# Linear attention and two MLPs on one core: a reciprocal-root activation in place of Ln and Exp, a shorter norm step, and four of the second batch's products in plain float32

## The chip, the cores and the metric

The kernel runs on one core of a Trainium2 chip. The metric is the device time of one execution in microseconds (us), the median of the runs shown. Matmuls run on TensorE (PE), whose weight loads are listed apart (PEld). VectorE (DVE) and ScalarE (ACT) do the elementwise work and read the matmul results out of PSUM, GpSimd (POOL) does very little here, and SyncE (SP) issues most of the DMAs.

## The reference

```python
def _attn_ref(q, k, v, g_norm):                 # 8 batches, 8 heads, 576 tokens, head_dim 64
    kv = np.einsum('bhsd,bhse->bhde', k, v)
    out = np.einsum('bhsd,bhde->bhse', q, kv)
    rms = np.sqrt(np.mean(out * out, axis=-1, keepdims=True) + 1e-06)
    return (out / rms * g_norm).astype(np.float32)

def _moe_ref(x, w_in, w_out):                   # 4608 tokens, 512 -> 2048 -> 512
    h = x @ w_in
    beta = 1.0
    ...
    g = np.where(pos, h, np.where(neg, 0.0, (h + beta) ** 2 / (4.0 * beta)))
    return (g @ w_out).astype(np.float32)

def _moe2_ref(x, w_in, w_out):                  # the same sizes
    h = x @ w_in
    r = np.maximum(h, 0.0)
    g = r * r
    return (g @ w_out).astype(np.float32)
...
    x = np.ascontiguousarray(attn_out.transpose(0, 2, 1, 3)).reshape(B * S, H * D)
    x = _moe_ref(x=x, **moe_kwargs)
    return _moe2_ref(x=x, **moe2_kwargs)
```

The weights arrive as float64 words and are narrowed to float32 inside the kernel.

## The kernel before

A float32 product is made of three matmuls of a rounded type (float32r): each operand is split into a rounded part (hi) and the rest (lo), and `mm3` (L235 to L238) multiplies hi by hi, hi by lo and lo by hi into one PSUM bank. ACT casts the hi part, DVE subtracts it to get the lo part (`split`, L228 to L230; for weights L185).

The tokens are taken in blocks of 512 and, for layer 1, block b holds the tokens of batch b. A block has 16 steps f of 128 hidden units. `h_stage` multiplies x by `w_0_f` into `ph_b_f` (12 matmuls of 128x512), ACT and DVE make u from it (L705, L224, L707), `gs_b_f` is its split, and `out_stage` multiplies gs by `w_1_f` into four accumulators (`acc_b_0` to `acc_b_3`, 12 matmuls). Two PSUM banks named "h" take turns for ph. In block 0 each weight piece is narrowed just before it is used: ACT scales `raw` (L268), DVE builds the bits `d` (L270, L271), ACT casts `w` (L217) and DVE subtracts (L185).

Attention works on pairs of heads, four to a batch: k and v to `pkv` (L479), a transposed q times the kept kv matrix to `po` (two halves of 288 columns), squares of po, their sums over a head by a matmul with `ones` into `pr`, and the norm in `r_first` (batch 0) or `r_stage` (the others). There, ACT takes Ln of each half of pr from PSUM (L535, L602) and one Exp over 576 columns with scale -0.5 (L537, L604), so that y is a reciprocal root. ACT squares it into t (L224). DVE multiplies t by pr + 1e-6 (`newton`, L519, a half at a time); `norm` then forms (t - 3)*y (L522) and multiplies by o, the product scaled by g (L523). The result is split into the block's x.

Batch 0's attention runs ahead of everything; dummy matmuls (`pwarm`, L1157) stand between its steps on PE. The attention of batch b is hooked into block b-1, a pair about every seven steps, so batch 1's pairs 0 to 3 stand in block 0. For pairs 0 and 1 of batch 1 (`WHOLE`, L109) q and kv stay in plain float32 (L569, tile `kvw`) and so does the sum of squares; pairs 2 and 3 use the three-product form with `kvbd`. After the blocks of layer 1 come the passes of the rest, from about 714 us on.

The order of the instructions on each engine is set by a scheduler when the program is built; each engine takes its own in order. So an instruction that is added, taken out or released at another time in the schedule can change what stands beside it.

Of the kernel before, what the change touches and what calls it, by code (L numbers as in the profile page):

```python
# [15 lines left out]
BF16 = mybir.dt.bfloat16  # L16

LN_SCALE = 2.0**-44  # L20
LN2 = 0.6931471805599453

# [53 lines left out]
def linear_attention_rms_two_mlps(  # L78
# [16 lines left out]
    P = 128  # L95
# [12 lines left out]
    WAVE = 6  # L108
    WHOLE = ((1, 0), (1, 1))  # L109
    WARMS = ((0, 5), (6, 5), (8, 3), (12, 4), (14, 3), (20, 3), (26, 3))  # L110
    SPLITS = (10, 15, 24, 29, 32, 33)
# [77 lines left out]
    gvec = const.tile([P, 1], F32, name="gvec")  # L189
    lnb = const.tile([P, 1], F32, name="lnb")  # L190
    expb = const.tile([P, 1], F32, name="expb")
    halfb = const.tile([P, 1], F32, name="halfb")
# [274 lines left out]
    def kv_stage(b, *hps):  # L467
# [12 lines left out]
        for n, hp in enumerate(hps):  # L480
            for j in range(2):
                s = slice(j * D, (j + 1) * D)
                d = slice(n * P + j * D, n * P + (j + 1) * D)
                if b == 0:
                    copy(engine("kv_hi", b), kv0[s, hp, s], ps[s, d])
                    continue
                if (b, hp) in WHOLE:
                    copy(engine("kv_hi", b), kvw[s, hp % 2, s], ps[s, d])
                    continue
                t = kvbd[turn[b, hp] % len(kvbd)]  # L490
                copy(engine("kv_hi", b), t[s, 0, s], ps[s, d])
                nc.vector.tensor_tensor(t[s, 1, s], ps[s, d], t[s, 0, s].bitcast(F32), ALU.subtract)
# [27 lines left out]

    def norm(t, y, o):
        nc.vector.scalar_tensor_tensor(t, t, -3.0, y, op0=ALU.add, op1=ALU.mult)  # L522
        nc.vector.tensor_tensor(t, o, t, ALU.mult)  # L523

    marks = []

    def r_first(hp):
# [3 lines left out]
        for half in range(2):  # L531
            ps = bank(0, f"pr_0_{hp}_{half}")
            m = ps[:, :U]
            nc.tensor.matmul(m, ones.bitcast(F32), y[:, half], start=True, stop=True)  # L534
            nc.scalar.activation(y[:, half], m, AF.Ln, bias=lnb, scale=LN_SCALE)  # L535
            ms.append(m)
        nc.scalar.activation(y, y, AF.Exp, bias=expb, scale=-0.5)  # L537
        square(engine("y", 0), t, y)
        for half in range(2):
            newton(t[:, half], ms[half])  # L540
        norm(t, y, o)
        n = TB // 2
# [6 lines left out]
    def t_stage(b, hp):  # L549
        work = [ap1.tile([P, S], F32, tag=f"wk{n}", name=f"wk{n}_{b}_{hp}") for n in range(2)]  # L550
        if (b, hp) in WHOLE:
            qT = ap1.tile([P, S], F32, tag="hl0", name=f"qT_{b}_{hp}")
            nc.vector.transpose(qT, qs.pop((b, hp)))
            hl[b, hp] = (work, qT)
            return
# [7 lines left out]
    def o_stage(b, hp, half):  # L563
        work, parts = hl[b, hp]
        kv = kvbd[turn[b, hp] % len(kvbd)]
        c = slice(half * U, (half + 1) * U)
        if (b, hp) in WHOLE:
            ps = bank(b, f"po_{b}_{hp}_{half}")
            nc.tensor.matmul(  # L569
                ps[:, :U], kvw[:, hp % 2, :], parts[:, c], start=True, stop=True  # L570
            )
            nc.scalar.activation(work[0][:, c], ps[:, :U], AF.Square)
            scaled(engine("o", b), work[1][:, c], ps[:, :U], gvec)
            return
# [3 lines left out]
        s2 = og[b, hp]  # L578
        ps = bank(b, f"po_{b}_{hp}_{half}")
        mm3(ps[:, :U], lambda a: kv[:, a, :], lambda a: parts[a][:, c], True, True)  # L580
        nc.scalar.activation(s2[0][:, c], ps[:, :U], AF.Square)
        nc.scalar.activation(work[0][:, c], ps[:, :U], AF.Square)
        scaled(engine("o", b), work[1][:, c], ps[:, :U], gvec)
        if half == 1:
            s2.append(ap1.tile([P, S], F32R, tag="hl1", name=f"s2lo_{b}_{hp}"))
            lo = engine("sq_lo", b)
            lo.tensor_tensor(s2[1], work[0], s2[0].bitcast(F32), ALU.subtract)

    def r_stage(b, hp):
# [6 lines left out]
        for half in range(2):  # L596
# [3 lines left out]
            for n, (one, s2) in enumerate(products):  # L600
                nc.tensor.matmul(m, one, s2[:, c], start=n == 0, stop=n == len(products) - 1)  # L601
            nc.scalar.activation(y[:, c], m, AF.Ln, bias=lnb, scale=LN_SCALE)  # L602
            ms.append((c, m))
        nc.scalar.activation(y, y, AF.Exp, bias=expb, scale=-0.5)  # L604
        t = ap1.tile([P, S], F32, tag="wk2", name=f"t_{b}_{hp}")
        square(engine("y", b), t, y)
        for c, m in ms:
            newton(t[:, c], m)
        if b < LAST_B:
            norm(t, y, o)  # L610
            nc.gpsimd.tensor_copy(xrem[b][:, hp, :], t[:, TB:])
            split(xs[1, b][hp], t[:, :TB], "x", b)
            return
        xt = st.tile([P, TB], F32, tag="st", name=f"xt_{hp}")
        nc.vector.scalar_tensor_tensor(t, t, -3.0, y, op0=ALU.add, op1=ALU.mult)
        nc.vector.tensor_tensor(xt, o[:, :TB], t[:, :TB], ALU.mult)
        nc.vector.tensor_tensor(xrem[b][:, hp, :], o[:, TB:], t[:, TB:], ALU.mult)
        x_kept[hp] = xt
# [526 lines left out]

    nc.scalar.preload_act_table_set("natural_log_exp_and_others")
    load_first()
# [22 lines left out]
    nc.vector.tensor_scalar_mul(gvec, gvec, -0.5)  # L1170
    nc.vector.memset(lnb, LN_SCALE * 1e-6)
    nc.vector.memset(expb, -22.0 * LN2)
    nc.vector.memset(halfb, 0.5)
# [121 lines left out]
```

## Time and profile before

| | before |
|---|---|
| runs | 1556.57, 1558.22, 1556.27 us; median 1556.57 |
| profiled execution, its own time | 1556.74 us |
| its span | 1554.7 us |
| PE busy | 1545.8 us, 99% |
| DVE busy | 1131.3 us, 73% |
| ACT busy | 909.6 us, 59% |

The span is from the first to the last recorded work; some 2 us of the execution's time lie outside it. An engine that is busy for 99% of the span can get shorter only where it waits or by doing less. Where a wait is listed, the bracket behind a row gives the idle time before it and the engine and line that ended it. Consecutive instructions of an engine overlap, so the pitch (start to start) is less than the duration of one.

### The profile page before, as it was taken

Reading aid. Unit: us, or ns where it says so; the run is one execution under the profiler, and the core shown is the slowest. Engines: PE = TensorE matmul, PEld = TensorE weight load, DVE = VectorE, ACT = ScalarE, POOL = GpSimd, SP = SyncE. Lnnn points to the kernel's source line nnn. Section 1 sums busy time; section 2 is a strip of 40 time slices with the busy share of each in tenths; the row PEclk is TensorE's granted clock in tenths of the full one; section 3 lists DMA queues with packets and bytes.
Section 4 is the critical chain, followed back from the end, with each engine's and each line's share of the span. In section 5 each row is a group of like instructions: output and inputs, shape, how many; then the busy total and the mean of one; then the engine's idle time right before and its main releaser. Section 6 shows DMA issues by size and latency. Waiting matters only on the chain.

```text
span 1554.7 us, 22267 instructions
## 1 busy us (share of the span) xinstructions
PE 1545.8 (99%) x7727; PEld 1283.3 (83%) x7729; DVE 1131.3 (73%) x2000; ACT 909.6 (59%) x1713; POOL 20.5 (1%) x38
## 2 busy tenths in 40 slices
PE   9999999999999999999999999999999999999999
PEld 5787888888888888888888888888888888888898
DVE  6986886877877776754587559778965596558666
ACT  5977766767666676664355346456644463446354
POOL 0000000000000000000000000000000000000000
PEclk9999999999999999999999999999999999999999
DMA  9666899996877967935676867696876676877796
GB/s 288 197 216 187 278 319 279 304 313 197 274 250 238 284 208 227 293 98 172 193 245 194 227 213 246 197 238 200 259 227 204 205 238 197 241 248 224 212 392 249
DMA packets 327519, 368.22 MB, mean 237 GB/s; under 512 B 196976, under 2 KB 222576, under 8 KB 327408
## 3 DMA queue, kind: packets, MB, share of 16 engines
q1 hardware_dynamic: 295360, 308.60, 66.4%
q10 hardware_dynamic: 32048, 58.20, 9.9%
q8 instruction: 61, 1.00, 0.3%
q14 instruction: 50, 0.41, 0.1%
HBM read 282.59 MB, written 84.15 MB: 236 GB/s over the span
## 4 chain that ended last, share of the span: by engine, by line
PE 97%; ACT 1%; DVE 1%; issue 0%; DVEq 0%; ACTq 0%
PE po L878 27%; PE ph L878 27%; PE acc L238 20%; PE ph L238 19%; PE pkv L479 1%; PE po L238 1%; PE pr L601 1%; PE pwarm L1157 1%; ACT raw L268 0%; ACT w L217 0%; PE pr L534 0%; DVE t L519 0%; DVE w L185 0%; PE po L511 0%; DVE t L522 0%; PE po L569 0%
## 5 line engine op out<-in xcount | busy, mean ns | idle before, releaser
L878 PE MATMUL ph<-x,ws 128*128 128x512 f32 (+1 forms) x2016 | 422.4, 371 | 0.0
L878 PEld LDWEIGHTS ph<-x,ws 128*128 128x128 f32 x2016 | 355.8, 188 | 65.6
L878 PE MATMUL po<-t,ws 128*128 128x512 f32 x1680 | 381.6, 389 | 0.0
L878 PEld LDWEIGHTS po<-t,ws 128*128 128x128 f32 x1680 | 315.3, 188 | 65.5
L238 PE MATMUL ph<-x,w 128*128 128x512 f32 x1344 | 329.4, 392 | 1.3 <-ACT w L217 0.6
L238 PEld LDWEIGHTS ph<-x,w 128*128 128x128 f32 x1344 | 248.7, 188 | 54.3 <-ACT w L217 1.5
L807 DVE TENSOR_TENSOR t<-g,t 128x512 fp32r<-128x512 f32 (+1 forms) x288 | 183.3, 641 | 92.2 <-ACT t L217 84.6
L217 ACT CAST t<-g 128x512 fp32r<-128x512 f32 (+1 forms) x288 | 166.5, 585 | 101.8 <-PE po L878 50.2
L238 PE MATMUL acc<-gs,w 128*128 128x512 f32 x696 | 173.0, 392 | 1.5 <-DVE u L707 1.5
L238 PE MATMUL acc<-gs,wt 128*128 128x512 f32 x648 | 157.9, 391 | 0.0
L238 PEld LDWEIGHTS acc<-gs,w 128*128 128x128 f32 x696 | 128.6, 188 | 27.8 <-DVE u L707 1.9
L949 ACT ACTIVATE g<-h 128x512 f32<-128x512 f32 (+1 forms) x120 | 70.7, 589 | 119.8 <-DVE h L938 119.8
L238 PEld LDWEIGHTS acc<-gs,wt 128*128 128x128 f32 x648 | 120.1, 188 | 24.3
L705 ACT ACTIVATE u<-ph,halfb 128x512 f32<-128x512 f32 x112 | 77.2, 690 | 91.5 <-PE ph L238 89.1
L938 DVE CUSTOM_DVE_ANT_0 h<-ph,e 128x512 f32<-128x512 f32 (+1 forms) x120 | 76.4, 638 | 64.8 <-PE ph L878 57.3
L707 DVE SCALAR_TENSOR_TENSOR u<-u,ph 128x512 f32<-128x512 f32 x112 | 76.3, 681 | 54.2 <-ACT u L224 53.8
L928 DVE TENSOR_TENSOR e<-ph,e 128x512 f32<-128x512 f32 (+1 forms) x96 | 61.1, 643 | 50.2 <-PE ph L878 49.6
L230 DVE TENSOR_TENSOR gs<-u,gs 128x512 fp32r<-128x512 f32 x112 | 76.8, 686 | 22.2 <-ACT gs L217 21.8
L217 ACT CAST gs<-u 128x512 fp32r<-128x512 f32 x112 | 69.7, 622 | 37.5 <-DVE u L707 34.7
L224 ACT ACTIVATE u<-u 128x512 f32<-128x512 f32 x112 | 70.8, 632 | 1.4 <-ACT u L705 0.5
L217 ACT CAST x<-xr 128x512 fp32r<-128x512 f32 (+1 forms) x84 | 49.0, 586 | 36.0 <-DVE xr L858 17.5
L807 DVE TENSOR_TENSOR x<-xr,x 128x512 fp32r<-128x512 f32 (+1 forms) x84 | 53.1, 637 | 7.3 <-ACT x L217 7.3
(134 smaller groups left out, 1494.5 us busy)
## 6 DMA issues: line engine op xcount, KB each, us to landing
ws<-wsd SPq DMA_DIRECT2D x336, 512.0 KB, 4.2
wsd<-s ACTq DMA_DIRECT2D x96, 512.0 KB, 4.7
wt<-wsd SPq DMA_DIRECT2D x54, 512.0 KB, 5.4
raw<-in_moe_w_in_dram SPq DMA_DIRECT2D x32, 512.0 KB, 5.8
raw<-in_moe_w_out_dram SPq DMA_DIRECT2D x32, 512.0 KB, 6.2
xr<-x1d SPq DMA_DIRECT2D x36, 256.0 KB, 4.9
out_dram<-ov SPq DMA_DIRECT2D x142, 64.0 KB, 3.5
wsd<-w SPq DMA_DIRECT2D x17, 512.0 KB, 5.0
```

The lines of the kernel that those rows point to most:

```text
L217: return e.copy(dst, src)
L224: e.activation(dst, src, AF.Square)
L230: lo = engine(op + "_lo", phase).tensor_tensor(t[:, 1, :], src, t[:, 0, :].bitcast(F32), ALU.subtract)
L238: nc.tensor.matmul(dst, wt(a), xt(c), start=first and n == 0, stop=last and n == 2)
L479: nc.tensor.matmul(ps[s, d], lhs, rhs, start=c == 0, stop=c == MR)
L705: nc.scalar.activation(u, ps, AF.Relu, bias=halfb, scale=0.5)
L707: nc.vector.scalar_tensor_tensor(u, u, 1.0, ps, op0=ALU.min, op1=ALU.max)
L807: engine2(op + "_lo").tensor_tensor(t[:, 1, :], src, t[:, 0, :].bitcast(F32), ALU.subtract)
L878: nc.tensor.matmul(ps, wt(a), xt(c), start=first and n == 0 and i == 0, stop=last and n == len(lhs) - 1 and i == 2, skip_group_check=True,)
L928: nc.vector.tensor_tensor(e[i, p], bank, e[i, 1], ALU.add)
L938: nc.vector._custom_dve(TENSOR_ADD_SAT, out=h, in0=bank, in1=add, s0=float("inf"), s1=0.0)
L949: nc.scalar.activation(g, h, AF.Square)
```

## The change

Two edits. First, in the norm of every pair, Ln (two halves) and Exp give way to one function, `Abs_reciprocal_sqrt` with bias 1e-6, which ACT takes straight from pr in PSUM, a half at a time; the table set that is loaded at the start is named accordingly. The norm step is rearranged: o is multiplied by y as soon as y is there, beside ACT's square, and after `newton` a single operation forms (t - 3)*o. Second, for the pairs of `WHOLE_O` (all four of batch 1) q and kv stay float32 in the product po; for pairs 2 and 3, which are new in it, the squares are still split in two parts. The second edit takes the ACT cast and the DVE difference of q and of kv out for these two pairs and makes each half of po one float32 matmul in place of three.

```diff
-    lnb = const.tile([P, 1], F32, name="lnb")
-    expb = const.tile([P, 1], F32, name="expb")
+    epsb = const.tile([P, 1], F32, name="epsb")
+    WHOLE_O = tuple((1, hp) for hp in range(NP))
...
-                if (b, hp) in WHOLE:
+                if (b, hp) in WHOLE_O:
                     copy(engine("kv_hi", b), kvw[s, hp % 2, s], ps[s, d])
...
-    def norm(t, y, o):
-        nc.vector.scalar_tensor_tensor(t, t, -3.0, y, op0=ALU.add, op1=ALU.mult)
-        nc.vector.tensor_tensor(t, o, t, ALU.mult)
+    def norm(dst, t, o):
+        nc.vector.scalar_tensor_tensor(dst, t, -3.0, o, op0=ALU.add, op1=ALU.mult)
...
@@ r_first (the same edit in r_stage)
-            nc.scalar.activation(y[:, half], m, AF.Ln, bias=lnb, scale=LN_SCALE)
+            nc.scalar.activation(y[:, half], m, AF.Abs_reciprocal_sqrt, bias=epsb)
             ms.append(m)
-        nc.scalar.activation(y, y, AF.Exp, bias=expb, scale=-0.5)
         square(engine("y", 0), t, y)
+        nc.vector.tensor_tensor(o, o, y, ALU.mult)
         for half in range(2):
             newton(t[:, half], ms[half])
-        norm(t, y, o)
+        norm(t, t, o)
...
@@ t_stage
-        if (b, hp) in WHOLE:
+        if (b, hp) in WHOLE_O:
             qT = ap1.tile([P, S], F32, tag="hl0", name=f"qT_{b}_{hp}")
             nc.vector.transpose(qT, qs.pop((b, hp)))
...
@@ o_stage
+        whole = (b, hp) in WHOLE_O
+        if whole:
             ps = bank(b, f"po_{b}_{hp}_{half}")
             nc.tensor.matmul(
                 ps[:, :U], kvw[:, hp % 2, :], parts[:, c], start=True, stop=True
             )
+        if (b, hp) in WHOLE:
             nc.scalar.activation(work[0][:, c], ps[:, :U], AF.Square)
             scaled(engine("o", b), work[1][:, c], ps[:, :U], gvec)
             return
...
-        ps = bank(b, f"po_{b}_{hp}_{half}")
-        mm3(ps[:, :U], lambda a: kv[:, a, :], lambda a: parts[a][:, c], True, True)
+        if not whole:
+            ps = bank(b, f"po_{b}_{hp}_{half}")
+            mm3(ps[:, :U], lambda a: kv[:, a, :], lambda a: parts[a][:, c], True, True)
...
-            s2.append(ap1.tile([P, S], F32R, tag="hl1", name=f"s2lo_{b}_{hp}"))
+            s2.append(ap1.tile([P, S], F32R, tag="hl0" if whole else "hl1", name=f"s2lo_{b}_{hp}"))
...
-    nc.scalar.preload_act_table_set("natural_log_exp_and_others")
+    nc.scalar.preload_act_table_set("abs_reciprocal_sqrt_and_small")
```

The order of the instructions moves with it. Two places are shown; a row is the line, the operation, out<-in and the shape. Lines of the changed kernel are 5 to 8 lower for the same statement.

On ACT in the attention of batch 0 (y_0, t_0 are pair 0's, y_1 pair 1's; L537 is the Exp), before:

```order
L535 ACTIVATE y_0_282<-pr_0_0_333,lnb 128x288
L268 ACTIVATE raw_0_0_151<-raw_0_0_151 128x512
L535 ACTIVATE y_0_282<-pr_0_1_336,lnb 128x288
L537 ACTIVATE y_0_282<-y_0_282,expb 128x576
L512 ACTIVATE y_1_348<-po_1_0_350 128x288
L209 ACTIVATE o_1_349<-po_1_0_350,gvec 128x288
L512 ACTIVATE y_1_348<-po_1_1_354 128x288
L224 ACTIVATE t_0_332<-y_0_282 128x576
L217 CAST w_0_0_300<-d_0_0_297 128x2x256
```

and now (L527 is the reciprocal root, L217 the square, L261 the scaling of raw weights):

```order
L527 ACTIVATE y_0_280<-pr_0_0_331,epsb 128x288
L261 ACTIVATE raw_0_0_150<-raw_0_0_150 128x512
L527 ACTIVATE y_0_280<-pr_0_1_334,epsb 128x288
L217 ACTIVATE t_0_330<-y_0_280 128x576
L261 ACTIVATE raw_0_1_152<-raw_0_1_152 128x512
L505 ACTIVATE y_1_345<-po_1_0_347 128x288
L202 ACTIVATE o_1_346<-po_1_0_347,gvec 128x288
L505 ACTIVATE y_1_345<-po_1_1_351 128x288
L527 ACTIVATE y_1_345<-pr_1_0_391,epsb 128x288
```

The square of pair 0 stands behind the second root at once and ahead of pair 1's squares of po, where it stood behind them; a scaling of raw weights moves ahead of pair 1, and the cast of w_0_0 behind pair 1's first root.

On ACT in block 0 where batch 1's pair 3 is worked on (s_1_3 and wk_1_3 are its squares and products, raw_0_14 to w_1_13 pieces of the weights), before:

```order
L217 CAST gs_0_13_1390<-u_0_13_1386 128x512
L217 CAST qT_1_3_1246<-qf_3_1245 128x576
L268 ACTIVATE raw_0_14_1027<-raw_0_14_1027 128x512
L581 ACTIVATE s_1_3_1316<-po_3_0_1317 128x288
L582 ACTIVATE wk_1_3_1243<-po_3_0_1317 128x288
L217 CAST w_0_14_1084<-d_0_14_1081 128x2x256
L268 ACTIVATE raw_1_13_1051<-raw_1_13_1051 128x512
L209 ACTIVATE wk_1_3_1244<-po_3_0_1317,gvec 128x288
L581 ACTIVATE s_1_3_1316<-po_3_1_1339 128x288
L582 ACTIVATE wk_1_3_1243<-po_3_1_1339 128x288
L209 ACTIVATE wk_1_3_1244<-po_3_1_1339,gvec 128x288
L217 CAST w_1_13_1255<-d_1_13_1252 128x2x256
```

and now:

```order
L210 CAST gs_0_13_1361<-u_0_13_1357 128x512
L576 ACTIVATE s_1_3_1293<-po_3_0_1291 128x288
L261 ACTIVATE raw_0_14_1013<-raw_0_14_1013 128x512
L577 ACTIVATE wk_1_3_1222<-po_3_0_1291 128x288
L202 ACTIVATE wk_1_3_1223<-po_3_0_1291,gvec 128x288
L576 ACTIVATE s_1_3_1293<-po_3_1_1312 128x288
L210 CAST w_0_14_1070<-d_0_14_1067 128x2x256
L261 ACTIVATE raw_1_13_1037<-raw_1_13_1037 128x512
L577 ACTIVATE wk_1_3_1222<-po_3_1_1312 128x288
L202 ACTIVATE wk_1_3_1223<-po_3_1_1312,gvec 128x288
L597 ACTIVATE wk_1_3_1222<-pr_3_0_1376,epsb 128x288
L261 ACTIVATE raw_0_15_1064<-raw_0_15_1064 128x512
```

raw_0_14 stood ahead of the first square of po_3_0 and now stands behind it, and w_1_13, which stood ahead of the logarithm of pr_3_0, now stands behind its root (it is the next row, behind raw_0_15).

On PE at the same place (gs_0_12 are the operands of block 0's thirteenth step; 12 matmuls of gs_0_11 stand between ph_0_13 and the first row), before:

```order
L238 MATMUL acc_0_0_848<-gs_0_12_1324,w_1_12_1174 128x512 x3
L238 MATMUL acc_0_1_849<-gs_0_12_1324,w_1_12_1174 128x512 x2
L238 MATMUL po_3_0_1317<-qT_1_3_1246,kvbd_130 128x288
L238 MATMUL po_3_1_1339<-qT_1_3_1246,kvbd_130 128x288
L238 MATMUL acc_0_1_849<-gs_0_12_1324,w_1_12_1174 128x512
L238 MATMUL acc_0_2_850<-gs_0_12_1324,w_1_12_1174 128x512 x2
```

and now:

```order
L231 MATMUL acc_0_0_841<-gs_0_12_1297,w_1_12_1156 128x512 x3
L231 MATMUL acc_0_1_842<-gs_0_12_1297,w_1_12_1156 128x512 x3
L231 MATMUL acc_0_2_843<-gs_0_12_1297,w_1_12_1156 128x512 x2
L562 MATMUL po_3_0_1291<-qT_3_1224,kvw 128x288
L562 MATMUL po_3_1_1312<-qT_3_1224,kvw 128x288
L231 MATMUL acc_0_2_843<-gs_0_12_1297,w_1_12_1156 128x512
L231 MATMUL acc_0_3_844<-gs_0_12_1297,w_1_12_1156 128x512 x3
```

The first matmul of po_3_0 stood behind 17 matmuls of acc that follow ph_0_13, and stands behind 20 now.

On DVE a little later (u_0_14 is made from ph_0_14 and sets its "h" bank free; t_3 is pair 3's norm), before:

```order
L185 TENSOR_TENSOR w_0_15_1150<-d_0_15_1147,w_0_15_1150 128x2x256
L271 SCALAR_TENSOR_TENSOR d_1_14_1292<-raw_1_14_1110,d_1_14_1292 128x512
L707 SCALAR_TENSOR_TENSOR u_0_14_1436<-u_0_14_1436,ph_0_14_1423 128x512
L185 TENSOR_TENSOR w_1_14_1295<-d_1_14_1292,w_1_14_1295 128x2x256
L270 TENSOR_SCALAR d_1_15_1366<-raw_1_15_1168 128x512
L519 SCALAR_TENSOR_TENSOR t_3_1414<-pr_3_0_1405,t_3_1414 128x288
L271 SCALAR_TENSOR_TENSOR d_1_15_1366<-raw_1_15_1168,d_1_15_1366 128x512
L519 SCALAR_TENSOR_TENSOR t_3_1414<-pr_3_1_1409,t_3_1414 128x288
```

and now (L512 is newton, L515 the new last step of the norm, L601 o*y):

```order
L601 TENSOR_TENSOR wk_1_3_1223<-wk_1_3_1223,wk_1_3_1222 128x576
L512 SCALAR_TENSOR_TENSOR t_3_1384<-pr_3_0_1376,t_3_1384 128x288
L179 TENSOR_TENSOR w_1_14_1270<-d_1_14_1267,w_1_14_1270 128x2x256
L263 TENSOR_SCALAR d_1_15_1337<-raw_1_15_1150 128x512
L512 SCALAR_TENSOR_TENSOR t_3_1384<-pr_3_1_1380,t_3_1384 128x288
L264 SCALAR_TENSOR_TENSOR d_1_15_1337<-raw_1_15_1150,d_1_15_1337 128x512
L515 SCALAR_TENSOR_TENSOR t_3_1384<-t_3_1384,wk_1_3_1223 128x576
L701 SCALAR_TENSOR_TENSOR u_0_14_1406<-u_0_14_1406,ph_0_14_1393 128x512
```

u_0_14 stood ahead of the whole norm of pair 3 and now stands behind all of it.

## Rows read from the trace of the kernel before

**Rows 1.** The page: busy time by engine, then the chain's shares by engine.

```profile
PE 1545.8 (99%) x7727; PEld 1283.3 (83%) x7729; DVE 1131.3 (73%) x2000; ACT 909.6 (59%) x1713; POOL 20.5 (1%) x38
...
PE 97%; ACT 1%; DVE 1%; issue 0%; DVEq 0%; ACTq 0%
```

**Rows 2.** Windows: stretch and its length, busy us (instructions) by engine, clock, DMA.

```profile
0.00:30.00 30.00, 27.25 (x171) 15.06 (x174) 18.02 (x49) 15.03 (x29) 2.80 (x12) 1.00 0.99 290
30.00:60.00 30.00, 27.72 (x131) 20.36 (x130) 27.92 (x51) 27.57 (x56) 0.87 (x2) 1.00 0.92 270
...
200.00:300.00 100.00, 100.00 (x525) 83.19 (x524) 78.58 (x146) 69.64 (x138) 2.09 (x4) 1.00 0.95 296
```

**Rows 3.** Timeline of PE in the head: start, length, idle before and its releaser.

```profile
53.84 0.97 PE L238 MATMUL acc<-gs,w 128*128 128x512 f32 x3 [1.51 <-DVE u L707]
```

**Rows 4.** Chain of waits from 8 to 54: start, us, what.

```profile
20.00 0.67 DVE t L523
...
29.42 0.78 ACT y L537
...
34.01 0.67 DVE t L523
...
38.00 0.63 ACT w L217
```

**Rows 5.** Lines by form, 0 to 150: count, busy us, mean ns, idle before.

```profile
L238 PE MATMUL po<-qT,kvbd 128*128 128x288 f32 x18 | 3.5, 304 | 0.0
L535 ACT ACTIVATE y<-pr,lnb 128x288 f32<-128x288 f32 x8 | 3.9, 501 | 3.7 <-PE pr L534 3.7
L569 PE MATMUL po<-qT,kvw 128*128 128x288 f32 x8 | 2.3, 412 | 0.0
```

**Rows 6.** Chain of waits, 54 to 57.

```profile
54.81 1.02 PE po L569 x4
```

**Rows 7.** Timeline of PE in block 0, 108 to 131.

```profile
108.98 2.88 PE L238 MATMUL ph<-x,w 128*128 128x512 f32 x12
111.70 4.02 PE L238 MATMUL acc<-gs,w 128*128 128x512 f32 x17
115.56 0.42 PE L238 MATMUL po<-qT,kvbd 128*128 128x288 f32 x2
115.83 0.85 PE L238 MATMUL acc<-gs,w 128*128 128x512 f32 x3
116.52 0.69 PE L238 MATMUL po<-qT,kvbd 128*128 128x288 f32 x4
117.04 1.08 PE L238 MATMUL acc<-gs,w 128*128 128x512 f32 x4
118.30 1.22 PE L238 MATMUL ph<-x,w 128*128 128x512 f32 x3 [0.18 <-ACT w L217]
...
127.53 2.20 PE L238 MATMUL ph<-x,w 128*128 128x512 f32 x9
```

**Rows 8.** Timeline of ACT, the same stretch.

```profile
115.28 0.67 ACT L268 ACTIVATE raw<-raw 128x512 f32<-128x512 f32 x1
117.03 0.41 ACT L581 ACTIVATE s<-po 128x288 fp32r<-128x288 f32 x1 [1.07 <-PE po L238]
117.33 0.41 ACT L582 ACTIVATE wk<-po 128x288 f32<-128x288 f32 x1
117.62 0.62 ACT L217 CAST w<-d 128x512 fp32r<-128x512 f32 x1
```

**Rows 9.** Timeline of DVE, the same stretch.

```profile
116.61 0.69 DVE L271 SCALAR_TENSOR_TENSOR d<-raw,d 128x512 int32<-128x512 int32 x1
118.28 0.69 DVE L185 TENSOR_TENSOR w<-d,w 128x512 fp32r<-128x512 f32 x1 [0.97 <-ACT w L217]
...
125.19 0.69 DVE L707 SCALAR_TENSOR_TENSOR u<-u,ph 128x512 f32<-128x512 f32 x1 [0.47 <-ACT u L224]
```

**Rows 10.** Timeline of ACT from the start.

```profile
0.73 1.28 ACT L1146 ACT_TABLE_LOAD   x1 [0.73 <-PEq L1273]
```

## What is predicted of the changed kernel, and from what

> **What bounds the kernel now.** I read the page's busy shares first, then its chain [rows 1]: PE is busy for 1545.8 of 1554.7 us and has 97% of the chain. So only two things can move the end: matmul time itself, and the few places where PE stands still or is filled with dummy matmuls. The windows say where these are [rows 2]: PE is busy 27.25 and 27.72 us in the first two stretches of 30 us, and 100.00 of 100.00 between 200 and 300 us, as in the stretches after it up to 1500. PE's clock is 1.00 in each of these windows, so it is no term here. From 30 to 60 us DVE and ACT are busy 27.92 and 27.57 of 30 us; between 200 and 300 us only 78.58 and 69.64 of 100. What the edit takes off ACT in the later blocks (one Exp for each pair) is therefore covered by PE's work and counts as nothing. If that cover were gone there, it could at most give back the duration of the Exp, 0.78 us [rows 4], for each of the 24 pairs of batches 2 to 7.
>
> The chain of waits in the head runs over ACT and DVE, not PE. It holds the last step of the norm of pair 1 (0.67 us at 20.00), the Exp of pair 2 (0.78 at 29.42) and the last step of pair 2 (0.67 at 34.01) [rows 4]. From 38.00 on it is a queue of weight casts and hidden activations on ACT that ends at PE's first acc matmul at 53.84, after an idle time of 1.51 us [rows 3]. That matmul is the clock of the head: from it on PE is full but for one small gap. The dummy matmuls count as busy, so the gain in the head isn't bounded by PE's idle time there, but by how much earlier that row can come.
>
> **Edit 1, the root and the norm.** For each pair two Ln of 288 columns at 0.501 us [rows 5] become two roots of the same shape, and the Exp goes. No row shows the root. All ACT rows with 288 columns lie between 0.41 (the squares, [rows 8]) and 0.501 us; I take the Ln's value, since both read PSUM and carry a bias tile. The bounds are the square's 0.41 and, far on the other side, the 0.78 of the 576-column Exp: -0.2 to +0.6 us for each pair.
>
> DVE keeps its number of operations, but o*y now lies beside ACT's square, so one operation of 0.67 us leaves each pair's chain. On the chain as it stands that is 0.67 + 0.78 + 0.67 = 2.1 us. The Exp of pair 0, also 0.78 us, stands ahead of pair 1's squares of po in ACT's order and falls out there, so at most some 2.9 us. What is late next? With pair 1's norm earlier, the copies of kv and qT for pair 2 stand behind more DVE work (the x split of pair 0 and newton of pair 1), so that po of pair 2 would be 1 to 2 us later than the roots alone would make it; it comes at about its old time. I walked through the new orders of ACT, DVE and PE with the durations of the old rows: newton of pair 2 comes some 2.6 us earlier, and the first acc matmul at about 51.3 in place of 53.84. I take **-2.5 us** for the head, with bounds of 0 (the copies of kv and qT take over the chain) and -4.
>
> **Edit 2, the float32 product of pairs 2 and 3.** A pair had six matmuls with a mean of 304 ns and gets two in float32, which the trace lists as four with a mean of 412 ns [rows 5]: 1.82 against 1.65 us of overlapping durations. On the chain the float32 pair takes 1.02 us [rows 6]. The two groups of pair 3 take from 115.56 to 115.83 and from 116.52 to 117.04 from start to start, 0.79 us [rows 7]. So from -0.1 to +0.25 us for a pair; I take +0.1, together **+0.2 us**, since the chain's figure has the ends that count. The casts and differences of q and kv that go lie beside PE's work.
>
> **What the new order does at pair 3.** This is the third term, and it has the other sign. In before, twelve matmuls take 2.72 us (108.98 to 111.70), 0.227 each [rows 7]. From 118.12, where PE wants w_0_14 (118.30 less its wait of 0.18), to ph_1_0 at 127.53 there are 24 matmuls of ph and 12 of acc, 8.16 us, and four of pr at some 0.13: 8.70 in 9.41 us, so that with the wait before has lost 0.9 us here.
>
> Now count from the end of ph_0_13 (111.70 in before) as zero. The first square of po_3_0 comes on ACT after 20 matmuls, 4.53, and half the product, 0.51: at 5.1. raw_0_14 stands behind it, starting 0.30 later (117.03 to 117.33, [rows 8]) and lasting 0.67, to 6.1. In before it was done at 115.95, 4.25 after the zero. DVE makes d from it, 0.69, and ACT works through three more 288-column operations meanwhile; the cast of w_0_14, 0.62, ends at 7.6 and its lo part, 0.69 [rows 9], at 8.3. PE wants them at 6.6 and, after two matmuls, 7.1. That is a wait of about 1.4 us. Behind it w_1_13 waits for the root of pr_3_0, which waits for the squares' lo part: I get a second wait of 0.55. Together 1.95 in place of 0.9: **+1.1 us**.
>
> The last piece is u_0_14, which sets the "h" bank of ph_1_0 free. In before it ended at 125.88, 1.65 us ahead of ph_1_0 [rows 7, 9]. Now it stands behind o*y, both newtons, w_1_14 and the new last step. Six DVE operations of 0.35 to 0.69 from the second root on bring its end to about 18.2 by my count, while PE wants the bank at 17.1. This may cost up to 1.1 us; such a count over a dozen steps errs by as much as that, and I take **+0.5**. Bounds for the whole place: 0 to +3.
>
> **The sum.** -2.5 + 0.2 + 1.1 + 0.5 = -0.7 us. The profiled execution took 1556.74 us with a span of 1554.7, so about 1556.0 is its counterpart. It stood 0.17 above the median of 1556.57, which leads to **1555.9**. The bounds of the terms add up to a range of -4.2 (the head's -4, the product's -0.2, nothing at pair 3) to +3.5.
>
> **Rivals.**
> *The head's gain passes whole.* The wait at pair 3 is not there, because everything that ACT and DVE do for block 0 has moved forward with the head. Then -2.5 + 0.2 = -2.3, about 1554.2, and down to 1552.4 if the head gives 4. For it: ACT is idle for 1.07 us ahead of the square in before [rows 8], so there is slack to absorb something. Against it: raw_0_14 is bound to po_3_0 by the order, and po_3_0 to PE, so it moves with PE and gains nothing from the head.
>
> *The queue at pair 3 takes more than the head gives.* ACT's square of po_3_0 holds up not only raw_0_14 but, through the roots, w_1_13, w_0_15, w_1_14 and w_1_15, and each is late by its own cast and lo part, 0.62 + 0.69 = 1.31 us. Four of these and the 1.4 of the first are 6.6 us; less the 0.9 of before, +5.7, and with the head's -2.5 and +0.2 that gives +3.4 us, 1560.0. It decides the sign once this place costs over 2.3 us more than in before. Against it: PE's own 12 matmuls, 2.72 us, lie between two pieces.
>
> *The table has to be changed.* Before loads one table, 1.28 us at the start [rows 10]. If Square, Copy or the weights' scaling weren't in the new one, every root would bring two loads: in the head 4 pairs by 2 by 1.28, 10 us on the chain, about 1567, and more in block 0. In the order of the changed kernel ACT has still a single load, which speaks against it. The Trainium skill ("ScalarE: Activation LUTs", "What ACT_TABLE_LOAD costs") puts a switch between sets at some 2.66 us with its drain, about twice the row's 1.28; by that the head alone would lose 21 us. No row here shows a switch.
>
> *Nothing shows.* The head's first acc matmul hangs on weights that are narrowed at their own pace, so that it stays at 53.84; only the product's +0.2 is left: 1556.8. Against it: ACT's queue starts at 38.00 with a cast that waits for a DVE queue, in which the norms stand.
>
> **Chances and range.** The forecast, with an own range of 1554.5 to 1557.5: 50%. The head whole: 27%. The queue at pair 3: 11%. Nothing: 10%. The table: 2%. About 0.2%, 3.1 us, is what a measurement of this kernel can tell from no change: below 1553.5 is faster, above 1559.7 slower. Of the head-whole case a good half lies below, with a little of the forecast: 18%. Above lie the table and much of the queue case: 10%. The rest, 72%, is within. The range of 1552.6 to 1559.2 leaves out about a tenth on either side.
>
> **What would show it.** Step one: the first acc matmul after the head at 51 to 51.6. Half a microsecond or less of gain there says that another chain took over. Step two: po of pairs 2 and 3 with four matmuls at about 1.0 us a pair. Step three: PE idle ahead of ph_0_14, about 1.4 us, with ACT's cast of w_0_14 as its releaser, a smaller one ahead of the acc matmuls of gs_0_13, and ph_1_0 waiting for DVE's L701. If PE is full through this place, the head's gain should stand in the result. The roots would show a mean of about 0.50 us; anything over 0.6, a second table load, or PE idle after block 0 would make the prediction wrong.

## The result: slower, by 0.73%

| | before | changed |
|---|---|---|
| median of the timed runs | 1556.79 us (6 runs) | 1568.62 us (6 runs, 1566.31 to 1570.34) |
| ratio | | 1.0073, interval 1.0060 to 1.0086 |
| profiled execution, its own time and span | 1556.74, 1554.7 | 1570.34, 1568.5 |
| PE, DVE, ACT busy | 1545.8, 1131.3, 909.6 us | 1549.9, 1127.5, 887.3 us |

The change costs 11.8 us, where a gain of 0.7 was forecast and 1559.2 was the upper end of the range. All line numbers below are those of the kernel named beside them. Each ratio below is to runs of before taken beside it (medians 1556.79 to 1557.04 us). Two runs of `e2_whole_only` (1939.83 and 2207.50 us, at a mean clock of 0.745 and 0.654) and one of before (4006.80 us) lie far off the others and are left out.

The page of the changed kernel, busy time and the chain by engine and by line, against [rows 1]:

```profile
PE 1549.9 (99%) x7725; PEld 1284.4 (82%) x7725; DVE 1127.5 (72%) x1993; ACT 887.3 (57%) x1679; POOL 13.4 (1%) x38
...
PE 91%; DVE 3%; DMA 3%; ACT 1%; issue 1%; SPq 0%; ACTq 0%; DVEq 0%
PE po L872 27%; PE ph L872 27%; PE acc L231 17%; PE ph L231 16%; DMA wf<-wsd 2%; PE pkv L472 1%; PE po L231 1%; PE pr L596 1%; PE pwarm L1151 0%; DVE d L264 0%; DVE u L701 0%; DMA x1d<-ev 0%; DMA v<-in_v_dram 0%; DMA wsd<-s 0%; DVE w L179 0%
```

ACT does 22 us less, as the edit says, and nothing of that arrives. PE's share of the chain fell from 97 to 91%, and a transfer that the prediction never named, `wf<-wsd`, now has 2% of it. The windows of the changed kernel tell where (columns as in [rows 2]):

```profile
0.00:30.00 30.00, 25.32 (x155) 13.39 (x155) 14.89 (x41) 11.52 (x23) 2.39 (x12) 0.89 1.06 255
200.00:300.00 100.00, 98.72 (x518) 81.94 (x517) 79.10 (x149) 66.13 (x132) 1.88 (x4) 1.00 1.02 311
300.00:400.00 100.00, 98.07 (x513) 80.94 (x512) 76.61 (x144) 66.32 (x133) 2.46 (x5) 1.00 0.87 267
500.00:600.00 100.00, 96.02 (x503) 78.78 (x502) 77.24 (x145) 66.62 (x133) 1.94 (x4) 1.00 0.79 241
```

The first 30 us lost 1.9 us of PE's work and some of its clock (0.89 where before had 1.00), and three of the stretches that were full to the hundredth are so no longer (400 to 500 and 600 to 700 us still are). All of it lies ahead of the passes, which begin at 703 us in before and at 717 now: from their first matmul to the end before and the changed kernel take 851.5 us each. So the loss can be laid out along PE's marks, in the two profiled executions:

| stretch on PE | before | changed | difference |
|---|---|---|---|
| start to the first sum of squares, `pr` | 12.15 | 15.40 | +3.25 |
| from there to the first acc | 41.69 | 41.15 | -0.5 |
| from there to the end of ph_0_13 | 57.86 | 58.47 | +0.6 |
| from there to ph_1_0 (pair 3) | 15.83 | 18.42 | +2.6 |
| from there to the passes | 575.6 | 583.6 | +7.9 |

Up to rounding the five make the difference of the two spans, 13.8 us. The profiled execution of the changed kernel is the slowest of its six; a second profile (`after_again`, 1566.97 us) has 13.58 in the first row and 582.1 in the last, and the other three within 0.4 us. The 0.6 of the third row is one wait, which no profile of the old norm has:

```profile
60.48 0.75 PE L596 MATMUL pr<-wk,ones 128*128 128x288 f32 x2 [0.41 <-ACT wk L202]
```

The largest difference is the last. This is what PE waited for between 130 and 1560 us in the changed kernel (us in total, times, longest); before has no such row at all:

```profile
PE po L231 <- ACT qT L210: 5.0, 3, 2.6
PE ph L231 <- DVE u L701: 2.1, 3, 1.1
PE pkv L472 <- DVE t L512: 0.8, 1, 0.8
```

Two of these waits, followed back by the chain (start, us, what), in the changed kernel:

```profile
201.64 6.79 DMA wf<-wsd
208.43 0.02 issue
208.46 0.06 DVE wf L334
...
209.06 0.78 DVE qf L550
209.84 0.02 issue
209.87 0.68 ACT qT L210
210.55 0.04 issue
210.59 0.40 PE po L231
...
315.78 5.33 DMA wt<-wsd
321.11 0.12 issue
321.22 0.69 DVE wf L334
321.92 0.61 DVE u L701
322.52 0.04 issue
322.57 1.65 PE ph L231 x6
```

`wf` holds nine pieces of layer 1's output weights that are read back from DRAM (L316 in before, L309 now); DVE adds their two halves (`prep_join`, L341 and L334), and what is made of the sums goes back to DRAM for the passes. No work of blocks 1 to 6 needs it. But DVE takes its instructions in order: it stands still until the transfer lands, and behind it stand the transposition of q (first case) and u (second case), for which PE waits. (The trace puts the end of the second wait down to a load of `wt`, which SP issued 1.7 us behind that of `wf`.) PE's own rows at the two places have 1.28 and 1.07 us before them; with four later ones, behind such sums on DVE in the same way, it is 7.1 us, the 0.76 of pair 3 not counted (4.4 in the second profile).

In before, too, DVE waits for these transfers; by the engine's waits from 130 to 715 us, before first, then the changed kernel:

```profile
DVE wf L341 <- DMA wf<-wsd: 16.8, 7, 3.5
```

```profile
DVE wf L334 <- DMA wf<-wsd: 16.0, 6, 4.3
DVE wf L334 <- DMA wt<-wsd: 7.7, 1, 7.7
```

16.8 us of waiting cost before nothing, since they lie where DVE is ahead of PE. The order of DVE's instructions shows what moved. The u ahead of each of the nine sums is, in before, u_1_11, u_2_5, u_2_14, u_3_8, u_4_2, u_4_12, u_5_6, u_6_0, u_6_1; in the changed kernel u_1_11, u_2_5, u_2_12, u_3_6, u_4_0, u_4_9, u_5_2, u_5_13, u_5_14. The first stands behind the same u, but now ahead of q's transposition, which it followed. With the new norm the scheduler puts load and sum up to four steps earlier, and in both kernels most sums so soon behind their loads that DVE has to wait. The seventh pair of them, load on SP and sum on DVE, in before and in the changed kernel:

```profile
553.64 0.38 SPq L316 DMA_DIRECT2D wf<-wsd  x1
...
558.16 0.69 DVE L341 TENSOR_TENSOR wf<-wf 128x512 f32<-128x512 f32 x1 [2.54 <-DMA wf<-wsd]
```

```profile
542.87 0.41 SPq L309 DMA_DIRECT2D wf<-wsd  x1
...
549.64 0.69 DVE L334 TENSOR_TENSOR wf<-wf 128x512 f32<-128x512 f32 x1 [3.37 <-DMA wf<-wsd]
```

The first is followed by a norm that nobody waits for yet. The second stands ahead of a norm, two u and then qf, and ends in the dearest wait, PE's 2.60 at 559.44 for qT. The nine loads also take longer to land, 6.7 us in the middle in place of 5.1.

### The profile page after: what moved, and what is told of

The parts are those of the page before. It is cut to its first block, busy times and chain, and to the rows that moved or that the text cites. A ratio compares the mean times of both kernels' runs of the same rounds, so it can differ in the third digit from the quotient of the medians.

```text
span 1568.5 us, 22214 instructions
## 1 busy us (share of the span) xinstructions
PE 1549.9 (99%) x7725; PEld 1284.4 (82%) x7725; DVE 1127.5 (72%) x1993; ACT 887.3 (57%) x1679; POOL 13.4 (1%) x38
## 4 chain that ended last, share of the span: by engine, by line
PE 91%; DVE 3%; DMA 3%; ACT 1%; issue 1%; SPq 0%; ACTq 0%; DVEq 0%
PE po L872 27%; PE ph L872 27%; PE acc L231 17%; PE ph L231 16%; DMA wf<-wsd 2%; PE pkv L472 1%; PE po L231 1%; PE pr L596 1%; PE pwarm L1151 0%; DVE d L264 0%; DVE u L701 0%; DMA x1d<-ev 0%; DMA v<-in_v_dram 0%; DMA wsd<-s 0%; DVE w L179 0%
## 5 line engine op out<-in xcount | busy, mean ns | idle before, releaser
L217 ACT ACTIVATE u<-u 128x512 f32<-128x512 f32 x112 | 70.8, 632 | 1.1
```

The lines of the kernel that those rows point to most:

```text
L217: e.activation(dst, src, AF.Square)
```

## Experiments

The first questions are which of the two edits does it, and whether the sums are the place.

**One edit at a time.** `e1_root_only` is the changed kernel with float32 q and kv for pairs 0 and 1 alone; `e2_whole_only` is before with the second edit alone.

```
-    WHOLE_O = tuple((1, hp) for hp in range(NP))
+    WHOLE_O = WHOLE                               # e1
```

> The changed kernel with edit 2 undone: pairs 2 and 3 of batch 1 have the three-product form again, root and shorter norm step stay. Theory A (the root edit lets the scheduler put the sums over wf, weights read back from DRAM, on DVE one to four steps earlier, where DVE waits for their DMA and holds up qT and u behind it): wf stands behind the same u as in the changed kernel, so PE idles some 5 to 8 us between 200 and 600 us and the time is 1563 to 1569. Rival R (the float32 product and the new order in block 0 shift everything behind): PE full between 200 and 600, 1555 to 1558.

> The kernel before with edit 2 alone: Ln, Exp and the old norm step, and float32 products for all of batch 1. Theory A: wf stands where it stood before, to one step, so PE stays full between 200 and 600 us and the time is 1556 to 1558. Rival R: PE idle in blocks 2 to 5 as in the changed kernel, over 1563.

Measured: the root alone 1566.46 us, ratio 1.0059 (1.0047 to 1.0071); the float32 product alone 1558.52, ratio 1.0008 (0.9999 to 1.0017). The root and its norm bring most of the loss, and with it the early sums (the same nine u as in the changed kernel); the second edit alone leaves them within a step of before's places and costs at most 2.6 us, 1.2 by its ratio, which the interval doesn't tell from nothing.

**The loads of wf taken out.** `e3_no_wf_load` leaves out the nine transfers and adds halves of other weights, which are in SBUF already (what is made of them is then another number).

```
-                    nc.sync.dma_start(t, kept_whole(1, 1, f))
...
-                d, w = t[:, :, 0, :], t
+                d, w = t[:, :, 0, :], wo[L, f % (NF - TAIL)].bitcast(F32)
```

> The changed kernel without the nine loads of wf; the sums are made from other weights that lie in SBUF, so that part of the second product's weights is wrong. Theory A: nothing on DVE waits for these DMAs, PE's idle time between 200 and 600 us (7.1 in the profile of the changed kernel) falls below 1, and the time falls by 6 to 8 to about 1561. Rival D (the DMAs are slower throughout, whatever the order; wf is only where it shows first): other waits take their place, PE still idles 3 or more there, over 1565.

> The changed kernel once more. If the late first k and v (the first pr on PE at 15.4 us in place of 12.2) belongs to the kernel, the head is as late again: first acc matmul at 56 to 57. If it's chance, first pr at 12 to 13 and first acc at 51 to 54. Time 1566 to 1570 either way, PE idle between 200 and 600 us of 5 to 8.

`after_again` is the changed kernel once more: 1568.91 us, ratio 1.0075 (1.0062 to 1.0088). Its first `pr` came at 13.58 us and its first acc at 54.41, between the two cases expected. Without the loads: 1560.44, ratio 1.0017 (1.0008 to 1.0025), so 8.5 us less. PE's waits from 130 us on in that run:

```profile
PE ph L231 <- DVE u L700: 0.8, 1, 0.8
PE pr L595 <- DVE s2lo L581: 0.5, 1, 0.5
```

The first is ph_1_0, at pair 3; of the changed kernel's other waits none is left. The edit also takes nine transfers off the queues, and the scheduler orders other instructions of DVE and ACT anew, so it doesn't yet tell the place of the sums from the traffic.

**Function or order.** `e5_ln_for_root` keeps the changed kernel's order and puts Ln, and the old table, where the root stands (the norm is then another number).

```
-            nc.scalar.activation(y[:, half], m, AF.Abs_reciprocal_sqrt, bias=epsb)
+            nc.scalar.activation(y[:, half], m, AF.Ln, bias=epsb)
...
-    nc.scalar.preload_act_table_set("abs_reciprocal_sqrt_and_small")
+    nc.scalar.preload_act_table_set("natural_log_exp_and_others")
```

> The changed kernel with Ln in place of the root (the norm is then wrong) and the table set of before; the order of the instructions on every engine is that of the changed kernel. Four profiles with the root have the first pr on PE at 13.6 to 15.4 us, the two without it at 12.2 and 12.9. If the table set or its function is what makes the first loads late (theory S), the first pr comes at 12 to 13, the mean clock is back at 1.0, and the time falls by 1.5 to 3 to about 1566. If the late loads come with the order or the rest of the program (rival), first pr at 13.5 or later, clock 0.998, time 1567 to 1570.

1568.74 us, ratio 1.0079 (1.0065 to 1.0093), the changed kernel's time, and the first `pr` comes at 15.18 us, so that the late start isn't the root's or its table's either. The root as a function costs nothing; its order does.

**The sums put back.** `e6_join_behind_u` leaves every load and puts each sum behind the u that it followed in before.

```
+    BEHIND = [(1, 11), (2, 5), (2, 14), (3, 8), (4, 2), (4, 12), (5, 6), (6, 0), (6, 1)]
...
-            nc.vector.tensor_tensor(d, w[:, :, 0, :], w[:, :, 1, :], ALU.add)
...
+                with tc.issue_after(u_last[BEHIND.pop(0)]):
+                    nc.vector.tensor_tensor(d, w[:, :, 0, :], w[:, :, 1, :], ALU.add)
```

> The changed kernel complete, with one thing pinned: each sum over wf is queued on DVE behind the u behind which it stood in before. Theory A: the loads still land when they land, but u and qT no longer stand behind the wait, so PE's idle time between 200 and 600 us falls from 7.1 (4.6 in the second profile) below 1 and the time falls by 6 to 9 to about 1560, as without the loads. Rival D (slower DMAs): the wait moves to another place, the time falls by less than 3.

1560.05 us (1558.61 to 1564.28), ratio 1.0022 (1.0013 to 1.0031): 8.6 us less than the changed kernel with the same transfers. The loads stayed early (the seventh at 541.47, its sum at 555.76 without a wait), so that most sums now find their weights there. From ph_1_0 to the passes the profile takes 575.3 us, and that of `e3_no_wf_load` 575.0; before takes 575.6, the changed kernel's two profiles 583.6 and 582.1. This shows that DVE's standing at the sums, and not the traffic, costs most of the loss. (Other instructions of DVE and ACT change places here too; but the waits that are gone are those behind the sums.) One such wait is left, since the first sum still stands ahead of q's transposition of batch 2's first pair. PE in `e6_join_behind_u`, its only idle row from 131 to 700 us:

```profile
206.60 0.40 PE L231 MATMUL po<-qT,kvbd 128*128 128x288 f32 x1 [0.69 <-ACT qT L210]
```

**Pair 3 put back.** `e7_block0_order` adds to that what the prediction blamed in block 0: raw_0_14's scaling goes ahead of the square of po_3_0, and pair 3's norm is hooked one step f later (two of the half-steps that the hooks count), so that u_0_14 comes ahead of it.

```
+        if (b, hp, half) == (1, 3, 0):
+            with tc.issue_after(scaled_raw[1, 0, 14]):
+                nc.scalar.activation(s2[0][:, c], ps[:, :U], AF.Square)
...
-            slots.append((s + 6, r_stage, b, hp))
+            slots.append((s + (8 if (b, hp) == (1, 3) else 6), r_stage, b, hp))
```

> As e6_join_behind_u, and at pair 3 of block 0 the first square of po_3_0 is queued behind the scaling of raw_0_14, and the norm of pair 3 is hooked one step later, which puts u_0_14 ahead of it on DVE. Theory B (the order at pair 3 costs 2.6 us from the end of ph_0_13 to ph_1_0, 18.4 against 15.8): the stretch is back at 16.3 or less and the time is 2 to 2.5 below e6_join_behind_u, about 1558. Rival: PE waits for something else there, less than 1 is gained.

1557.22 us (1556.03 to 1558.28), ratio 1.0001 (0.9992 to 1.0010): 2.8 us less than `e6_join_behind_u`, and before's time. From the end of ph_0_13 to ph_1_0 it takes 16.08 us (18.41 in `e6_join_behind_u`) without a wait. In this build the first wf sum also comes behind both of DVE's steps on that q, so the wait of 0.69 at 206.60 is gone too; the 2.8 hold both. (PE's only wait behind 130 us is now one of 0.69 at 272.62, for a newton.)

`e11_raw_only` keeps only the ACT half of that edit.

> The sums over wf stay pinned behind u, as in e6_join_behind_u (1.0022), and of block 0's two mendings only one is kept: raw_0_14's scaling goes ahead of s_1_3 on ACT; u_0_14 stays behind the norm on DVE, as in the changed kernel. Theory A (each of the two edits carries the part of pair 3 that its waits show): ph_0_13's end to ph_1_0 comes to about 17.6 us, between e6's 18.4 and e7_block0_order's, the wait of ph_1_0 on u_0_14 (0.76) stays, and the time is 1558.4 to 1559.4. Theory B (the ACT order alone carries it): 1557.2 as e7_block0_order. Theory C (the u on DVE alone carries it): 1560.0 as e6_join_behind_u.

1560.49 us (1558.53 to 1563.28), ratio 1.0020 (1.0012 to 1.0029), theory C's time. In the trace, though, the place behaves as theory A says: 17.63 us from ph_0_13's end to ph_1_0, and the wait on u_0_14 is the only one left there, though grown from 0.76 to 1.33. PE's row with it, and its next idle row:

```profile
130.60 3.06 PE L231 MATMUL ph<-x,w 128*128 128x512 f32 x12 [1.33 <-DVE u L714]
```

```profile
208.89 0.40 PE L231 MATMUL po<-qT,kvbd 128*128 128x288 f32 x1 [2.36 <-ACT qT L210]
```

The 0.8 us won at pair 3 are lost again at the first wf sum, where `e6_join_behind_u` lost 0.69 and this profile loses 2.36. One profile (the slowest of the 11 runs) doesn't show that it is so in all; how the 2.8 us split is left open.

**The late start.** The change takes two constants of one column out and puts one in. As the program is laid out, this moves nearly every tile in SBUF by 32 bytes, off the multiples of 64 on which before has them. `e8_pad32` gives the changed kernel one unread column more, which moves the tiles back; `e9_before_shift32` makes of before's two columns one tile, which shifts before's.

```
+    padb = const.tile([P, 1], F32, name="padb")          # e8
...
-    lnb = const.tile([P, 1], F32, name="lnb")             # e9
-    expb = const.tile([P, 1], F32, name="expb")
+    biases = const.tile([P, 2], F32, name="biases")
+    lnb, expb = biases[:, 0:1], biases[:, 1:2]
```

> The changed kernel with one more [128,1] constant, which nothing reads. Each such constant takes 32 bytes of a partition; the change has one fewer of them than before, so in it every tile behind them starts 32 bytes lower (k_0_0 at 188128 in place of 188160), at odd multiples of 32 bytes where before had multiples of 64. The extra constant puts them back. Theory M (DMAs into SBUF at odd multiples of 32 bytes are slower): the first pr comes at 12 to 13 us in place of 13.6 to 15.4, the mean clock is 1.0, the landing of the wf loads is back from 6.7 (median) to some 5 us, and the time falls by 4 to 8, to 1561 to 1565, with part of the idle time between 200 and 600 us left, since the sums over wf still stand early. Rival (the late start is the program's, not the address's): first pr at 13.5 or later, time 1567 to 1570.

> The kernel before with its two bias constants in one tile, which moves every tile behind them 32 bytes lower; nothing else. Theory M: first pr at 13.5 to 15.5, mean clock under 1.0 in most runs, time 1558 to 1561, with PE mostly full between 200 and 600 us because the sums over wf stand later there. Rival: 1556 to 1557.5 and first pr at 12 to 13.

The second load of v on SP's queue (start, us, line), in before and then in the changed kernel:

```profile
3.68 2.27 SPq L422 DMA_DIRECT2D v<-in_v_dram  x1
```

```profile
3.69 3.66 SPq L415 DMA_DIRECT2D v<-in_v_dram  x1
```

In `e8_pad32` it is 2.30 us long, in `e9_before_shift32` 3.06. The window from 4 to 8 us of before, the changed kernel, `e8_pad32` and `e9_before_shift32`, one fence each; the last number is the GB/s:

```profile
4.00:8.00 4.00, 4.00 (x31) 1.65 (x29) 0.00 (x0) 0.00 (x0) 0.00 (x0) 1.00 1.19 303
```

```profile
4.00:8.00 4.00, 1.92 (x21) 0.90 (x19) 0.00 (x0) 0.00 (x0) 0.00 (x0) 1.00 1.27 173
```

```profile
4.00:8.00 4.00, 3.60 (x31) 1.62 (x29) 0.00 (x0) 0.00 (x0) 0.00 (x0) 1.00 1.19 302
```

```profile
4.00:8.00 4.00, 3.15 (x22) 1.45 (x21) 0.00 (x0) 0.00 (x0) 0.00 (x0) 1.00 1.29 193
```

Within a pair the order of DVE, ACT and POOL is the same but for the memset of the unread column, so the 32 bytes are what moves 302 or 303 GB/s to 193 or 173. All nine profiles of shifted kernels have that load at 3.04 to 3.66 us and the first `pr` at 13.4 to 15.4 us; the five others 2.27 to 2.59 and 12.1 to 12.9. In time: `e8_pad32` 1563.91 us, ratio 1.0042 (1.0028 to 1.0055), 4.7 less than the changed kernel; `e9_before_shift32` 1558.03, ratio 1.0005 (0.9996 to 1.0013), no difference from before that can be told (at most 2.0 us by its interval).

Does the start have a price of its own? `e10_order_pad32` is `e7_block0_order` with that column, `e12_join_pad32` is `e6_join_behind_u` with it.

> The kernel of e7_block0_order with the extra constant. Theory M with A and B: the start is back at 12 to 13 us, PE full from block 0 on, and the shorter head (0.5 to 0.9 us from first pr to first acc) is what remains: 1554.5 to 1556, below both kernels. Rival: no change from e7_block0_order, 1557.

> e6_join_behind_u with the unread constant of e8_pad32, so that tiles stand at multiples of 64 bytes again, the sums over wf stay pinned and block 0's order is the changed kernel's. Theory A (the earlier start is worth its own part whatever else is mended): first pr at 12.0 to 13.0 us and 1558.3 to 1559.0. Theory B (what the alignment gave in e8_pad32 came only through the sums over wf that wait for DMAs): 1559.8 to 1560.3, with the first pr just as early.

1558.06 us against 1557.22 without it (ratios 1.0003, 0.9994 to 1.0012, and 1.0001); 1559.97 against 1560.05 (ratios 1.0016, 1.0007 to 1.0025, and 1.0022). The 1554.5 to 1556 expected of the first didn't come: with the sums in their places the column gives nothing that can be measured, though the first `pr` comes at 12.57 and 12.66 us in place of 13.80 and 13.42. So the 4.7 us of `e8_pad32` come for the larger part by way of the sums: in its trace PE waits 3.7 us from 130 us on, in the changed kernel's two 7.9 and 5.2. The price of the sums and that of the shift don't add; either mending takes part of the same waits.

Where does the earlier start go? In `e12_join_pad32` the first acc comes 0.8 us earlier than in `e6_join_behind_u` (52.36 and 53.15), the first matmul of the passes at the same time (705.34 and 705.32), with no wait between that the other lacks. The lead goes little by little: from ph_6_0 to ph_6_14, where PE waits in none of the profiles, it takes 84.80 us in all five unshifted ones and 84.69 in all nine shifted ones. From ph_1_0 to the passes that makes 576.05 against 575.30 us here, 576.17 against 575.57 in `e10_order_pad32` and `e7_block0_order`, and 575.64 against 574.88 in before and `e9_before_shift32`. So the shift gives back a part of what it costs at the start; why matmuls follow one another a little faster with it isn't shown.

## Why the prediction was wrong

**The step that failed: "What the edit takes off ACT in the later blocks … is therefore covered by PE's work and counts as nothing."** The cover was true for what was removed, and was taken to hold for all that the removal lets move. PE stood at 100.00 of 100 us in before [rows 2] because DVE's waits for wf happened to lie where DVE was ahead. The prediction compared the orders in the head and at pair 3, not in blocks 1 to 6, where seven of the nine sums stood two to four steps earlier and the first had passed q's transposition. If the cover were gone, it counted only on a gain, the Exp's 0.78 us a pair. What the runs show in its place is 8.5 and 8.6 us of loss (`e3_no_wf_load`, `e6_join_behind_u`). None of the four rivals held it; of the signs that it gave for being wrong, "PE idle after block 0" is the one that came.

**The head, -2.5 forecast.** The first acc came at 56.55, not 51.3; from the first `pr`, which takes the late start out, it came 0.5 us earlier.

```profile
56.55 1.66 PE L231 MATMUL acc<-gs,w 128*128 128x512 f32 x6
```

The chain that took over is the one named under "What is late next?": po of pair 2 behind pair 1's newton. PE's rows there in the changed kernel, then in `e6_join_behind_u`:

```profile
24.25 0.81 PE L1151 MATMUL pwarm<-warm 128*128 128x512 bf16 x3 [1.16 <-DVE t L512]
25.30 1.01 PE L1151 MATMUL pwarm<-warm 128*128 128x512 bf16 x2 [0.25 <-DVE kv L212]
26.11 2.12 PE L504 MATMUL po<-qT,kv 128*128 128x288 f32 x4
```

```profile
22.28 0.81 PE L1158 MATMUL pwarm<-warm 128*128 128x512 bf16 x3 [1.17 <-DVE t L518]
...
23.82 1.24 PE L510 MATMUL po<-qT,kv 128*128 128x288 f32 x4
```

From 24 to 28 us the granted clock is 0.65 in the changed kernel (1.00 in before), behind these idle times, and po's four matmuls take 2.12 us. In `e6_join_behind_u` PE stands still as long, but its clock is 1.00 from 22 to 28 us, and the four take 1.24. All eleven profiles with the new norm have this idle time of 1.16 or 1.17 us. In nine of them the clock falls behind it, and from the first `pr` to the first acc they take 40.8 to 41.2 us; in `e6_join_behind_u` and `e12_join_pad32` it stays at 1.00, and they take 39.7, which is 2.0 less than before. So the shorter norm is worth 2.0 of the 2.5 forecast, and the fall of the clock takes 1.1 to 1.4 of that back. What decides whether it falls isn't shown. The step that failed here is "PE's clock is 1.00 in each of these windows, so it is no term here"; in the head it is one, behind PE's new idle time.

**The start, no term at all.** The first `pr` comes 3.25 us later in this profile and 1.43 in the second, by 32 bytes; the prediction took everything ahead of the first norm as untouched. In time the shift by itself has no price that could be measured.

**Pair 3, +1.6 forecast, +2.6 in the trace, and up to 2.8 in time.** Mechanism and place are right. PE's rows in the changed kernel, against [rows 7]:

```profile
115.02 4.70 PE L231 MATMUL acc<-gs,w 128*128 128x512 f32 x20
119.55 1.13 PE L562 MATMUL po<-qT,kvw 128*128 128x288 f32 x4
120.31 1.31 PE L231 MATMUL acc<-gs,w 128*128 128x512 f32 x4
122.00 0.40 PE L596 MATMUL pr<-s,ones 128*128 128x288 f32 x1 [0.38 <-ACT wk L202]
122.80 1.69 PE L231 MATMUL ph<-x,w 128*128 128x512 f32 x5 [0.41 <-ACT w L210]
...
126.86 1.45 PE L231 MATMUL acc<-gs,w 128*128 128x512 f32 x5 [0.36 <-ACT w L210]
...
133.44 1.88 PE L231 MATMUL ph<-x,w 128*128 128x512 f32 x7 [0.76 <-DVE u L701]
```

All three waits foreseen are there, for w_0_14, w_1_13 and the bank behind u_0_14, with 0.41, 0.36 and 0.76 in place of 1.4, 0.55 and 0.5, and one more ahead of them for pr. The brackets make 1.91 us and understate the loss: a single matmul's row is 0.39 long, the pitch in a full row 0.227 (20 matmuls from 115.02 to 119.55), so by these rows each break costs an estimated 0.16 more than its bracket. The place needs both edits for this: the stretch takes 16.66 us with the first alone (`e1_root_only`) and 16.56 with the second alone (`e2_whole_only`), in place of 15.83 in before and 18.42 with both. ACT's order is the one predicted, raw_0_14 behind the first square (compare [rows 8]):

```profile
120.30 0.41 ACT L576 ACTIVATE s<-po 128x288 fp32r<-128x288 f32 x1 [2.35 <-PE po L562]
120.60 0.65 ACT L261 ACTIVATE raw<-raw 128x512 f32<-128x512 f32 x1
```

**The float32 product, +0.1 a pair forecast.** The sign was off: pair 3's takes 0.76 us from start to start (119.55 to 120.31 in the rows above), where before needed 0.79 [rows 7]. The chain's 1.02 counted an end that overlaps the next matmul.

**The root's price was right.** It was taken at Ln's 0.501 us; by lines, eight of them in the first 150 us:

```profile
L527 ACT ACTIVATE y<-pr,epsb 128x288 f32<-128x288 f32 x8 | 4.0, 501 | 2.8 <-PE pr L526 2.8
```

The rival of a second table had no part: the changed kernel loads one, and `e5_ln_for_root`, with the old one, has the same time. The Trainium skill's 2.66 us for a switch ("ScalarE: Activation LUTs", "What ACT_TABLE_LOAD costs") couldn't be met, since no run here switches.

With the sums and pair 3's order mended (`e7_block0_order`), the kernel is even with before, and not 2.3 us below it, as the forecast's terms for head and product alone would have it; no version beats before by more than can be measured. Its profile, whose clock fell in the head too, tells where that went: the first `pr` comes 1.65 us later than in before, the head gives 0.75, and block 0 takes 0.6 more behind the first acc and 0.25 more at pair 3.

## What to carry to other kernels

Where a scheduler sets the order, work that is removed off the critical path isn't free until it is known what moves into its place: list, for each in-order engine, the instructions that wait for a transfer, and compare what stands ahead of them in both orders over the whole program, not only where the edit is. A long wait that costs nothing in the profile of before is a warning, not a comfort. And compare the first 10 us of two traces before explaining the rest: a constant that comes or goes can shift nearly every tile. Where a change makes PE stand still, look at the granted clock behind the break too: it can cost as much again as the break itself.

## What was not expected of the hardware

Shifting the tiles in SBUF by 32 bytes, off multiples of 64, took the loads of the first microseconds from 302 or 303 GB/s to 173 or 193 between 4 and 8 us, in both kernels and both ways (297 to 305 in the five unshifted profiles, 173 to 204 in the nine shifted ones). One column of a constant is enough for it. Later it isn't seen: from 200 to 300 us the changed kernel moves 311 GB/s shifted and 308 unshifted (`e8_pad32`), before 298 shifted (`e9_before_shift32`) and 296 unshifted. Whether it is the address of the destination, or another thing that goes with it, wasn't tried.

After PE idled for 2.08 us at the start of the changed kernel, waiting for v, its granted clock was 0.57 in the window from 8 to 12 us, near the lower of the two levels (1.2 of 2.4 GHz); before, without that break, has 1.00 there. `e5_ln_for_root`, with a break of 2.06 us, shows the same fall; the seven other shifted profiles, with breaks of 0.85 to 1.31 us for the same load, have 1.00 behind them. Yet behind the 1.16 us at about 21 to 24 us it fell in nine profiles of eleven.
